# Attention head pipeline: where the split and low parts of the queries and keys of the head two further on stand among the query tiles

## Chip, core and metric

The kernel runs on one core of a Trainium2 chip. The metric is the device time in microseconds of one execution, as a median of several runs. One execution was taken with the hardware profiler; all rows and times of single instructions come from it.

Engines are named as in the profile: PE is TensorE (matrix products), PEld its weight loads, DVE is VectorE, ACT is ScalarE, POOL is GpSimd, SP is SyncE, which issues the transfers.

## Reference

The program is an attention stage, a mixture of experts on its output, and a gated product. Only the first is touched here:

```python
q_bucket = np.sum((np.einsum('bhsd,dk->bhsk', q, proj) > 0) * powers, axis=-1)   # and k_bucket alike
mask = q_bucket[:, :, :, None] == k_bucket[:, :, None, :]
scores = np.where(mask, scale * np.matmul(q, k.transpose(0, 1, 3, 2)), -1000000000.0)
attn = np.exp(scores - np.max(scores, axis=-1, keepdims=True))
attn = attn / (np.sum(attn, axis=-1, keepdims=True) + 1e-09)
return np.matmul(attn, v)
```

There are 2 x 8 heads, sequences of 768, head size 64, float32 throughout. The experts (8, with argmax routing) and the gated product (1536 wide) follow on 1536 tokens.

## The kernel before

**Stages.** The attention stage takes the first third of the span; the experts and the gated product follow. The attention runs over 16 heads (0 to 15) of six query tiles of 128 rows. Its main loop (line 676) makes one pass for each tile, `g = 6 h + t`; "pass t of head h" below is that pass. The loop is a pipeline written out by hand: within pass (h, t)

- TensorE first makes the scores of the *next* tile (`scores`, lines 158 and 159, four products into one PSUM tile `s`), then side work (the products of the previous head's probabilities with V, `av`, line 200, in passes 1, 3 and 5; the hash products of the next head, line 128, in pass 1; the output product of the head before the previous one, line 238, in pass 4), then the transposes of this tile's probabilities in two halves of three (`tp`, line 185). Passes 0 and 2 hold scores and transposes alone.
- VectorE takes the smallest score of the next tile (`mm`, line 164) and makes from it the scale and bias of the exponential (`sb`, line 165, 128x2 values).
- ScalarE makes the exponential `p` of the next tile (line 172), which waits for `sb`. The table `K` says at which of three positions in a pass it is issued: position 0 (ahead of the transposes) in passes 1, 3 and 5, position 2 (behind them) in passes 0, 2 and 4.
- The transposed probabilities are copied out of PSUM to `pt` by ScalarE (line 189) or VectorE (line 191, in passes 1, 2 and 4 for the second half). `tp` has two PSUM buffers, so a half of a tile waits until the same half of the tile before is copied.

Every engine works through its instructions in the order in which the program issues them.

**The split.** Scores are needed to float32 accuracy, and the products run on a format that keeps fewer bits. So queries and keys (`x`, both stacked twice along the partitions) are split into a rounded part and a remainder. For head h + 2, during head h, `split_a(h + 2, i)` (line 100) makes the rounded part on ScalarE, `tq` for queries (i = 0) and `tk` for keys (i = 1), one instruction each (line 103). `split_b(h + 2, i)` (line 107) makes the remainder: for queries VectorE's `bq` (line 115) and a copy on GpSimd (line 116); for keys a subtraction `bk` (line 118) and a copy (line 119), both on GpSimd. The results are first read one head later, by the scores issued in pass 5 of head h + 1.

**Other work around it.** `hash_codes` (line 140) takes the hash products of head h + 1 at position 0 of pass 1: VectorE's `code` (line 142), then four transfers by SP (line 147) that put the codes into rows of `tq` and `tk`. At the end of a head VectorE copies `av` to `o` and forms the reciprocal sums (lines 220 to 225). In pass 4 it scales the output product (`lp`, line 247; `x_all`, line 248), and GpSimd adds `lp` to the router's logits `lg` (line 250; VectorE for the last two heads of a batch). From pass 2 of head 10 on, VectorE also has the router's steps of the first half of the tokens.

**What sets the order.** The entries `sa` and `sb` of `K` list, for queries and keys, the pass and position at which `split_a` and `split_b` are issued; `side` (line 733) looks them up:

```python
K = {..., 'sa': ((2, 2), (4, 1)), 'sb': ((3, 2), (4, 2)), ...}
```

So `tq` is issued at the end of pass 2, `bq` and its copy at the end of pass 3, `tk` in the middle of pass 4 and `bk` with its copy at the end of pass 4.

Of the kernel before, what the change touches and what calls it, by code (L numbers as in the profile page):

```python
# [21 lines left out]
N, DM, E, FF, F2 = 1536, 512, 8, 1024, 1536  # L22
C = 224
GR = ((0, 6), (6, 4), (10, 2))
K = {'se': (2, 0, 2, 0, 2, 0), 'se0': (0, 1, 2, 1, 1, 2), 'ev': (0, 0, 0, 1, 0, 1, 0, 0, 0, 1, 0, 0), 'avl': (), 'oul': 0, 'hml': 0, 'hc': ((0, 0), (0, 2), (1, 1), (2, 1)), 'sa': ((2, 2), (4, 1)), 'sb': ((3, 2), (4, 2)), 'ext': (1, 0, 2, 4, 7, 8), 'hm0': 0, 'hc0': ((1, 0), (1, 2), (3, 0), (4, 1))}
C_ID, C_TRI, C_THR, C_REV, C_TOK, C_IOTA, C_BASE, C_SLOT = 0, 128, 256, 258, 266, 278, 279, 287
CW = C_SLOT + C
FAR = 1024.0
# [4 lines left out]
def attn_moe_kernel(ctx: ExitStack, tc: tile.TileContext, xin, cst, projd, wblk, wmoe, w2in, out):  # L33
# [29 lines left out]
    pos = const.tile([128, 12], F32, name="pos")  # L63
# [24 lines left out]
    NHD = NB * NH  # L88
# [4 lines left out]
    def load(h, first=()):  # L93
        X[h] = xp.tile([128, 2 * S], F32, tag="x", name="x")
        for i in range(2):
            after(nc.sync.dma_start(out=X[h][:, i * S:(i + 1) * S], in_=xin[h, :, i * S:(i + 1) * S]), first)
        V[h] = vp.tile([128, NT, D], F32, tag="v", name="v")
        nc.sync.dma_start(out=V[h], in_=xin[h, :, 2 * S:].rearrange("p (k d) -> p k d", d=D))
# [24 lines left out]
    def hash_mm(h, order=range(4)):  # L123
        p = (ps_m if h or 2 in order else ps_a).tile([128, 512], F32, tag="m" if h or 2 in order else "a", name="m")
        for j in order:
            i = j // 2
            hp_[h, j] = p
            PE.matmul(
                p[32 * j:32 * j + 32, :384], pst[:, 32 * i:32 * i + 32], X[h][:, j * 384:(j + 1) * 384],
                start=True, stop=True, skip_group_check=True,  # L130
            )
# [19 lines left out]
    def scores(g):  # L151
        h, t = divmod(g, NT)
        p = ps_s.tile([128, 2, 512], F32, tag="s", name="s")
        st[g] = p
        qs = slice(t * 128, t * 128 + 128)
        for c in range(2):
            sl = slice(c * 384, c * 384 + 384)
            PE.matmul(p[:, c, :384], T[h, 0][:76, qs], T[h, 1][:76, sl], start=True, stop=False)  # L158
            PE.matmul(p[:, c, :384], B[h, 0][:, qs], B[h, 1][:, sl], start=False, stop=True)  # L159

    def smax(g):
        m = mm[:, g % 4]
        sb = sm.tile([128, 2], F32, tag="sb", name="sb")
        DVE.tensor_reduce(out=m[:, 1:2], in_=st[g][:, :, :384], axis=AX.XY, op=ALU.min)  # L164
        DVE.scalar_tensor_tensor(  # L165
            out=sb, in0=m[:, 1:2].to_broadcast([128, 2]), scalar=BIG / 2, in1=m, op0=ALU.is_le, op1=ALU.mult
        )
        scl[g], nbs[g] = sb[:, 0:1], sb[:, 1:2]
# [9 lines left out]
    def tposes(g, half):  # L178
# [8 lines left out]
        src = ps[:, :384].rearrange("p (a b) -> p a b", a=3)  # L187
        if K["ev"][2 * t + half] == 0:
            ACT.activation(o, src, ACTF.Copy)  # L189
# [5 lines left out]
    def av_step(h, k):  # L195
        if k == 0:
            av[h] = ps_a.tile([128, 512], F32, tag="a", name="av")
        v = V[h][:, k]
        for c in range(2):
            PE.matmul(  # L200
                av[h][c * 64:(c + 1) * 64, :384], v, PT[h][:, k, c * 384:(c + 1) * 384],
                start=(k == 0), stop=(k == NT - 1), skip_group_check=True,
            )
# [261 lines left out]
    def w_load(n, part):  # L465
        if n < 64:
            RAW[n, part] = wraw.tile([128, 512], F32, tag=f"wr{part}", name=f"wr{part}")
            nc.sync.dma_start(out=RAW[n, part], in_=wmoe[n // 8, n % 8, :, part * 512:(part + 1) * 512])
# [126 lines left out]
    with tc.manual_schedule():  # L595
# [49 lines left out]
        def set_up(k):  # L645
            if k == 0:
                split_b(1, 0)
                POOL.tensor_copy(held, pt_[0][:, 0:1])
            elif k == 1:
                split_b(1, 1)  # L650
            elif k == 2:
                POOL.memset(oh, 0.0)
                zero = wraw.tile([128, 512], F32, tag="wr0", name="zero")
                POOL.memset(zero, 0.0)
                zeros.append(zero)
                DVE.tensor_copy(tri, cs[:, C_TRI:C_TRI + 128])
            elif k == 5:
                DVE.tensor_scalar(
                    out=tokc.bitcast(I32)[:, :, 0], in0=cs[:, C_TOK:C_TOK + 12], scalar1=-float(E * C), scalar2=None,
                    op0=ALU.add,  # L660
                )
                DVE.tensor_scalar(
                    out=base2, in0=cs[:, C_BASE:C_BASE + 8], scalar1=1.0 / 128, scalar2=None, op0=ALU.mult
                )
# [6 lines left out]
        extra = {}  # L671
        for at, f in zip(K["ext"], acts):
            extra.setdefault(divmod(at, NT), []).append(f)
        NG = NHD * NT
        qa, qb = (0, 4), (4, 2)
        for g in range(NG):
            h, t = divmod(g, NT)
            if t == 1 and h + 3 < NHD:
                load(h + 3)
            if g + 1 < NG:  # L680
                scores(g + 1)
                smax(g + 1)
            if g < NT:
                set_up(g)
            if 2 * NT <= g < 2 * NT + (E * C + N) // 256:
                for i in (g - 2 * NT,):
                    nc.sync.dma_start(
                        out=xr[i * 256:(i + 1) * 256].rearrange("(p r) d -> p r d", p=128),
                        in_=zeros[0].unsqueeze(1).to_broadcast([128, 2, 512]),
                    )  # L690
            if g == 6 * NT:
                for n in range(4):
                    for part in range(2):
                        w_load(n, part)
            if g == 10 * NT + 1:
                r = router(0)
                todo = [r["s1"], r["s1b"], None, lambda: (r["s2"](), r["s2c"]()), r["s2b"], r["s4"], r["s4b"]]
                for f in r["sc"]:
                    todo += [f, None]
                todo += [r["s4c"], r["s3"], r["s5"]]  # L700
            early, late = [], []
            if h < L:
                if t == (1 if h else 0):
                    early.append(lambda: hash_mm(h + 1))
                if h:
                    for k in AV_AT.get(t, ()):
                        early.append(lambda k=k: av_step(h - 1, k))
                if h > 1 and t == 4:
                    (late if K["oul"] else early).append(lambda: o_out(h - 2))
            elif t < 3:  # L710
                av_step(h - 1, 2 * t)
                av_step(h - 1, 2 * t + 1)
                if t == 0:
                    o_out(h - 2)
                if t == 2:
                    o_evac(h - 1)
            elif t == 3:
                o_out(h - 1)
            else:
                k = 3 * (t - 4)  # L720
                av_group(h, qa, (k, k + 1, k + 2))
                if t == 5:
                    o_evac(h, qa)
            for f in early:
                f()
            if h and h < L and t == 5 and not K["avl"].count(5):
                o_evac(h - 1)
            if g > 10 * NT + 1 and todo:
                f = todo.pop(0)
                if f:  # L730
                    f()

            def side(pos):
                if g + 1 < NG and K["se" if 0 < h < L else "se0"][t] == pos:
                    sexp(g + 1)
                for i in range(2):
                    if h + 2 < NHD and K["sa"][i] == (t, pos):
                        split_a(h + 2, i)
                    if h + 2 < NHD and K["sb"][i] == (t, pos):
                        split_b(h + 2, i)  # L740
                if h < L and (t, pos) == (1, 0):
                    hash_codes(h + 1)

            side(0)
            tposes(g, 0)
            side(1)
            tposes(g, 1)
            for f in late:
                f()
            if h and h < L and t == 5 and K["avl"].count(5):  # L750
                o_evac(h - 1)
            side(2)
            for f in extra.get((h - L + 1, t), ()):
                f()
# [578 lines left out]
```

## Time and profile before

| | |
|---|---|
| median of three runs | 756.61 us (755.6, 756.61, 760.02) |
| the profiled execution | 756.17 us, of which the span of instructions is 754.3 us |
| TensorE busy | 725.7 us, 96% of the span |
| VectorE, ScalarE, GpSimd busy | 528.4, 435.9, 281.1 us |
| TensorE's granted clock | 0.998 of full speed |

The span runs from the first to the last instruction of the program. A busy TensorE is not TensorE at its best, because products overlap and their ends are modelled; how long a pass of the loop takes is read from the starts of its scores (line 158), from one pass to the next. Idle time of the other engines costs nothing by itself. A wait is put down to what came last by the profile.

### The profile page before, as it was taken

The numbers are of one execution on the slowest core, as the hardware profiler recorded it, in microseconds if no ns is written. First come the engines' busy times: TensorE is split into PE (matmuls) and PEld (weight loads), VectorE is DVE, ScalarE is ACT, GpSimd is POOL, SyncE is SP. The second block draws the span as 40 slices with busy tenths as digits, with TensorE's granted clock in tenths as the row PEclk, the third lists the DMA queues.
The fourth block names the chain that finished last, engine by engine and source line by source line (L and its number), as shares of the span: only waits on it lengthen the run. The fifth ranks groups of instructions, "written<-read, shape, count | busy, mean of one in ns | idle before, by whom it ended". The sixth has DMA issues, their size and how long they took to land.

```text
span 754.3 us, 13409 instructions
## 1 busy us (share of the span) xinstructions
PE 725.7 (96%) x4621; PEld 619.7 (82%) x4622; DVE 528.4 (70%) x1033; ACT 435.9 (58%) x945; POOL 281.1 (37%) x319
## 2 busy tenths in 40 slices
PE   8899999999999999999999999999999999999995
PEld 6566666666666689999999999999999998999994
DVE  6777777777877677777778885687767246656641
ACT  5877677776678635666667764444553434344331
POOL 4332223321444256221221104353434476565543
PEclk9999999999999999999999999999999999999999
DMA  6356251112411018778898663646463322212102
GB/s 233 117 200 247 94 189 57 57 57 72 151 36 61 15 70 265 225 223 203 235 353 259 211 197 126 223 155 222 154 222 114 112 100 83 84 44 83 57 1 87
DMA packets 49594, 107.37 MB, mean 142 GB/s; under 512 B 8096, under 2 KB 11504, under 8 KB 47984
## 3 DMA queue, kind: packets, MB, share of 16 engines
q1 hardware_dynamic: 46848, 99.94, 40.8%
q0 software_dynamic: 2304, 6.31, 2.3%
q8 instruction: 38, 0.62, 0.4%
q14 instruction: 36, 0.29, 0.1%
q10 hardware_dynamic: 368, 0.20, 0.1%
HBM read 82.76 MB, written 22.56 MB: 140 GB/s over the span
## 4 chain that ended last, share of the span: by engine, by line
PE 82%; ACT 5%; DVE 5%; issue 3%; DMA 2%; POOL 2%; ACTq 0%; SPq 0%; DVEq 0%; POOLq 0%
PE tp L185 9%; PE av L200 8%; PE y L934 5%; PE acc L1056 4%; PE acc L1055 4%; PE acc L1057 4%; PE s L159 3%; PE s L158 3%; PE h L896 3%; PE h L895 3%; PE h L894 3%; ACT p L172 3%; PE y L935 3%; PE abb L894 2%; PE aba L895 2%
## 5 line engine op out<-in xcount | busy, mean ns | idle before, releaser
L172 ACT ACTIVATE p<-s,sb 128x768 f32<-128x768 f32 x96 | 94.8, 988 | 33.7 <-DVE sb L165 21.1
L164 DVE TENSOR_REDUCE mm<-s 128x1 f32<-128x768 f32 x96 | 91.6, 955 | 27.3 <-PE s L159 25.9
L185 PEld LDWEIGHTS tp<-cs,p 128*128 128x128 f32 x576 | 62.9, 140 | 52.8 <-ACT p L172 24.3
L853 POOL TENSOR_TENSOR pc<-t,pc 128x256 fp32r<-128x256 f32 x86 | 74.7, 892 | 83.3 <-ACT pc L852 83.3
L185 PE MATMUL tp<-cs,p 128*128 128x128 f32 x576 | 83.3, 281 | 16.6 <-ACT pt L189 11.0
L478 DVE TENSOR_TENSOR wl<-wr,wh 128x512 fp32r<-128x512 f32 x125 | 81.3, 689 | 10.0 <-ACT wh L477 5.5
L189 ACT ACTIVATE pt<-tp 128x384 f32<-128x384 f32 x144 | 65.4, 488 | 32.6 <-PE tp L185 32.6
L477 ACT ACTIVATE wh<-wr 128x512 fp32r<-128x512 f32 x128 | 73.8, 624 | 6.8 <-DMA wr<-wmoe 5.9
L934 PE MATMUL y<-hl,wh 128*128 128x448 f32 x224 | 74.9, 378 | 0.2
L158 PE MATMUL s<-tk,tq 76*128 76x384 f32 x192 | 73.1, 381 | 0.3 <-DVE tq L135 0.3
L894 PE MATMUL h<-xh,wh 128*128 128x224 f32 x256 | 71.4, 279 | 0.5 <-ACT wh L477 0.3
L896 PE MATMUL h<-xh,wl 128*128 128x224 f32 x256 | 70.6, 276 | 0.2 <-DVE wl L478 0.2
L895 PE MATMUL h<-xl,wh 128*128 128x224 f32 x256 | 70.2, 274 | 0.3 <-DVE xl L412 0.3
L200 PE MATMUL av<-pt,v 128*64 128x384 f32 x360 | 68.1, 499 | 0.0
L159 PE MATMUL s<-bk,bq 128*128 128x384 f32 x192 | 65.1, 339 | 0.0
L116 POOL CAST bq<-tq 64x768 fp32r<-64x768 f32 x15 | 21.2, 1414 | 112.9 <-ACT tq L103 98.4
L935 PE MATMUL y<-hl,wl 128*128 128x224 f32 x224 | 59.5, 266 | 0.0
L1055 PE MATMUL acc<-h,gh 128*128 128x512 f32 x144 | 56.7, 394 | 0.4 <-ACT gh L1041 0.4
L1056 PE MATMUL acc<-l,gh 128*128 128x512 f32 x144 | 56.8, 394 | 0.0
L1057 PE MATMUL acc<-h,gl 128*128 128x512 f32 x144 | 56.6, 393 | 0.0
L865 POOL TENSOR_TENSOR l<-t,h 128x512 fp32r<-128x512 f32 x24 | 31.0, 1293 | 64.7 <-ACT h L864 64.7
L894 PEld LDWEIGHTS h<-xh,wh 128*128 128x128 f32 x256 | 48.9, 191 | 1.7 <-ACT wh L477 0.5
(225 smaller groups left out, 1868.1 us busy)
## 6 DMA issues: line engine op xcount, KB each, us to landing
wr<-wmoe SPq DMA_DIRECT2D x128, 256.0 KB
r<-w2in SPq DMA_DIRECT2D x12, 1536.0 KB
x<-xin SPq DMA_DIRECT2D x30, 384.0 KB
w<-t SPq DMA_DIRECT2D x36, 256.0 KB
t<-w SPq DMA_DIRECT2D x36, 256.0 KB
xr<-zero SPq DMA_DIRECT2D x13, 512.0 KB
xg<-xr SPq DMA_DIRECT2D x14, 256.0 KB
v<-xin SPq DMA_DIRECT2D x16, 192.0 KB
```

The source lines that it names most:

```text
L158: PE.matmul(p[:, c, :384], T[h, 0][:76, qs], T[h, 1][:76, sl], start=True, stop=False)
L159: PE.matmul(p[:, c, :384], B[h, 0][:, qs], B[h, 1][:, sl], start=False, stop=True)
L164: DVE.tensor_reduce(out=m[:, 1:2], in_=st[g][:, :, :384], axis=AX.XY, op=ALU.min)
L172: ACT.activation(p.rearrange("p (c n) -> p c n", c=2), st.pop(g)[:, :, :384], ACTF.Exp, scale=scl.pop(g), bias=nbs.pop(g), accum_out=sums[ ...
L185: PE.transpose(ps[:, j * 128:(j + 1) * 128], pt_[g][:, k * 128:(k + 1) * 128], ident)
L200: PE.matmul(av[h][c * 64:(c + 1) * 64, :384], v, PT[h][:, k, c * 384:(c + 1) * 384], start=(k == 0), stop=(k == NT - 1), skip_group_check= ...
L894: PE.matmul(ps, wh, xh, start=first, stop=False)
L895: PE.matmul(ps, wh, xl, start=False, stop=False)
L896: PE.matmul(ps, wl, xh, start=False, stop=last)
L934: PE.matmul(p, wh[:, w], hl, start=(f == 0), stop=False, skip_group_check=True)
L1055: PE.matmul(acc[i], h[:, w], wh, start=(f == 0), stop=False)
L1056: PE.matmul(acc[i], h[:, w], wl, start=False, stop=False)
```

## The change

The table `K` gets other entries for the splits, and the old ones stay under new names for head 0:

```diff
-'sa': ((2, 2), (4, 1)), 'sb': ((3, 2), (4, 2)),
+'sa': ((0, 2), (2, 2)), 'sb': ((1, 0), (2, 2)), 'sa0': ((2, 2), (4, 1)), 'sb0': ((3, 2), (4, 2)),
...
-                    if h + 2 < NHD and K["sa"][i] == (t, pos):
+                    if h + 2 < NHD and K["sa" if h else "sa0"][i] == (t, pos):
                         split_a(h + 2, i)
-                    if h + 2 < NHD and K["sb"][i] == (t, pos):
+                    if h + 2 < NHD and K["sb" if h else "sb0"][i] == (t, pos):
                         split_b(h + 2, i)
```

In heads 1 to 13 `tq` is now issued at the end of pass 0, `bq` and its copy at the start of pass 1, `tk`, `bk` and its copy at the end of pass 2. Heads 14 and 15 have no split, and head 0 keeps its places. Instructions and transfers are the same in kind and number. TensorE's order is the same.

VectorE, pass 1 to pass 4 of one of the later heads, before (`mm` and `sb` are those of the next tile, `code` the hash codes, `pt` a transposed half):

```order
L164 TENSOR_REDUCE mm<-s 128x1
L165 SCALAR_TENSOR_TENSOR sb<-mm 128x2
L142 TENSOR_SCALAR code<-m,thr 128x384
L191 COPY pt<-tp 128x3x128
L164 TENSOR_REDUCE mm<-s 128x1
L165 SCALAR_TENSOR_TENSOR sb<-mm 128x2
L191 COPY pt<-tp 128x3x128
L164 TENSOR_REDUCE mm<-s 128x1
L165 SCALAR_TENSOR_TENSOR sb<-mm 128x2
L115 SCALAR_TENSOR_TENSOR bq<-x,tq 64x768
L164 TENSOR_REDUCE mm<-s 128x1
L165 SCALAR_TENSOR_TENSOR sb<-mm 128x2
```

The same stretch of VectorE after the change:

```order
L164 TENSOR_REDUCE mm<-s 128x1
L165 SCALAR_TENSOR_TENSOR sb<-mm 128x2
L115 SCALAR_TENSOR_TENSOR bq<-x,tq 64x768
L142 TENSOR_SCALAR code<-m,thr 128x384
L191 COPY pt<-tp 128x3x128
L164 TENSOR_REDUCE mm<-s 128x1
L165 SCALAR_TENSOR_TENSOR sb<-mm 128x2
L191 COPY pt<-tp 128x3x128
L164 TENSOR_REDUCE mm<-s 128x1
L165 SCALAR_TENSOR_TENSOR sb<-mm 128x2
L164 TENSOR_REDUCE mm<-s 128x1
L165 SCALAR_TENSOR_TENSOR sb<-mm 128x2
```

`bq` has moved from between the `sb` of tiles 4 and 5 to just ahead of `code`.

ScalarE, from the exponentials around the end of pass 2 to those of pass 5, before (`p` is an exponential, `pt` a copy of a transposed half):

```order
L172 ACTIVATE p,sums<-s,sb 128x768
L103 ACTIVATE tq<-x 128x768
L172 ACTIVATE p,sums<-s,sb 128x768
L189 ACTIVATE pt<-tp 128x3x128 x3
L103 ACTIVATE tk<-x 128x768
L172 ACTIVATE p,sums<-s,sb 128x768 x2
L189 ACTIVATE pt<-tp 128x3x128 x4
```

ScalarE from the end of pass 0 to pass 5, after:

```order
L172 ACTIVATE p,sums<-s,sb 128x768
L103 ACTIVATE tq<-x 128x768
L172 ACTIVATE p,sums<-s,sb 128x768
L189 ACTIVATE pt<-tp 128x3x128 x2
L172 ACTIVATE p,sums<-s,sb 128x768
L103 ACTIVATE tk<-x 128x768
L172 ACTIVATE p,sums<-s,sb 128x768
L189 ACTIVATE pt<-tp 128x3x128 x3
L172 ACTIVATE p,sums<-s,sb 128x768 x2
```

`tk` stands where `tq` stood, between the exponentials of tiles 3 and 4, `tq` stands between those of tiles 1 and 2, and the middle of pass 4 holds no split.

On GpSimd the keys' subtraction and copy now come ahead of the addition to the logits instead of behind it.

## Rows read from the trace of the kernel before

**Rows 1.** The page's first line: the span.

```profile
span 754.3 us, 13409 instructions
```

**Rows 2.** TensorE's waits, 30 to 232 us: us in total, times, longest.

```profile
PE tp L185 <- ACT pt L189: 11.0, 14, 1.2
```

**Rows 3.** TensorE in order of time, head 5: start, us, what [idle before].

```profile
93.01 0.42 PE L158 MATMUL s<-tk,tq 76*128 76x384 f32 x1
...
93.80 0.82 PE L185 MATMUL tp<-cs,p 128*128 128x128 f32 x6
94.38 0.42 PE L158 MATMUL s<-tk,tq 76*128 76x384 f32 x1
...
99.51 0.42 PE L158 MATMUL s<-tk,tq 76*128 76x384 f32 x1
...
102.47 0.42 PE L158 MATMUL s<-tk,tq 76*128 76x384 f32 x1
...
104.28 0.93 PE L185 MATMUL tp<-cs,p 128*128 128x128 f32 x6 [0.86 <-ACT pt L189]
104.96 0.42 PE L158 MATMUL s<-tk,tq 76*128 76x384 f32 x1
```

**Rows 4.** ScalarE in order of time, head 5.

```profile
91.60 0.99 ACT L172 ACTIVATE p<-s,sb 128x768 f32<-128x768 f32 x1 [0.59 <-DVE sb L165]
...
96.31 0.83 ACT L103 ACTIVATE tq<-x 128x768 fp32r<-128x768 f32 x1
...
102.76 0.99 ACT L172 ACTIVATE p<-s,sb 128x768 f32<-128x768 f32 x1 [1.10 <-PE tp L185]
```

**Rows 5.** VectorE in order of time, head 5.

```profile
91.56 0.68 DVE L142 TENSOR_SCALAR code<-m,thr 128x384 fp32r<-128x384 f32 x1
93.29 0.56 DVE L191 COPY pt<-tp 128x384 f32<-128x384 f32 x1 [1.05 <-PE tp L185]
...
96.67 0.16 DVE L165 SCALAR_TENSOR_TENSOR sb<-mm 128x2 f32<-128x2 f32 x1
97.17 0.95 DVE L115 SCALAR_TENSOR_TENSOR bq<-x,tq 64x768 fp32r<-64x768 f32 x1 [0.34 <-ACT tq L103]
...
99.31 0.16 DVE L165 SCALAR_TENSOR_TENSOR sb<-mm 128x2 f32<-128x2 f32 x1
99.39 0.26 DVE L247 TENSOR_TENSOR lp<-m,r 128x96 f32<-128x96 f32 x1
...
100.50 0.96 DVE L164 TENSOR_REDUCE mm<-s 128x1 f32<-128x768 f32 x1
101.50 1.15 DVE L165 SCALAR_TENSOR_TENSOR sb<-mm 128x2 f32<-128x2 f32 x1
102.57 0.55 DVE L220 COPY o<-av 128x384 f32<-128x384 f32 x1
```

**Rows 6.** GpSimd in order of time, head 5.

```profile
97.20 1.61 POOL L116 CAST bq<-tq 64x768 fp32r<-64x768 f32 x1 [9.40 <-ACT tq L103]
...
100.82 1.81 POOL L118 TENSOR_TENSOR bk<-x,tk 64x768 fp32r<-64x768 f32 x1 [0.63 <-POOL lg L250]
102.69 0.82 POOL L119 CAST bk<-tk 64x768 fp32r<-64x768 f32 x1
```

**Rows 7.** GpSimd, then VectorE, in order of time, pass 3 of head 2.

```profile
50.15 0.82 POOL L116 CAST bq<-tq 64x768 fp32r<-64x768 f32 x1 [9.40 <-ACT tq L103]
...
50.18 1.60 DVE L115 SCALAR_TENSOR_TENSOR bq<-x,tq 64x768 fp32r<-64x768 f32 x1 [0.41 <-ACT tq L103]
```

**Rows 8.** GpSimd, then VectorE, in order of time, head 10.

```profile
175.96 0.82 POOL L116 CAST bq<-tq 64x768 fp32r<-64x768 f32 x1 [9.38 <-ACT tq L103]
...
176.02 0.77 DVE L165 SCALAR_TENSOR_TENSOR sb<-mm 128x2 f32<-128x2 f32 x1
```

**Rows 9.** SP in order of time, head 5: the transfers of the keys' codes.

```profile
94.08 1.47 SPq L147 DMA_DIRECT2D tk<-code  x2
```

**Rows 10.** The query copies, line 116, 30 to 235 us: ns min/median/max, first and last start.

```profile
L116 POOL CAST bq<-tq x13: 817/1612/1636, 34.8 to 224.1; 64x768 fp32r<-64x768 f32 x13
```

More of the change, by code (lines that the diff above doesn't have):

```diff
@@ L24 @@
 GR = ((0, 6), (6, 4), (10, 2))
-K = {'se': (2, 0, 2, 0, 2, 0), 'se0': (0, 1, 2, 1, 1, 2), 'ev': (0, 0, 0, 1, 0, 1, 0, 0, 0, 1, 0, 0), 'avl': (), 'oul': 0, 'hml': 0, 'hc': ((0, 0), (0, 2), (1, 1), (2, 1)), 'sa': ((2, 2), (4, 1)), 'sb': ((3, 2), (4, 2)), 'ext': (1, 0, 2, 4, 7, 8), 'hm0': 0, 'hc0': ((1, 0), (1, 2), (3, 0), (4, 1))}
+K = {'se': (2, 0, 2, 0, 2, 0), 'se0': (0, 1, 2, 1, 1, 2), 'ev': (0, 0, 0, 1, 0, 1, 0, 0, 0, 1, 0, 0), 'avl': (), 'oul': 0, 'hml': 0, 'hc': ((0, 0), (0, 2), (1, 1), (2, 1)), 'sa': ((0, 2), (2, 2)), 'sb': ((1, 0), (2, 2)), 'sa0': ((2, 2), (4, 1)), 'sb0': ((3, 2), (4, 2)), 'ext': (1, 0, 2, 4, 7, 8), 'hm0': 0, 'hc0': ((1, 0), (1, 2), (3, 0), (4, 1))}
 C_ID, C_TRI, C_THR, C_REV, C_TOK, C_IOTA, C_BASE, C_SLOT = 0, 128, 256, 258, 266, 278, 279, 287
```

## Prediction

> **What bounds the kernel now.** I read the page first, then TensorE's own waits over the attention stage, then one head in order of time, engine by engine. The span is 754.3 us [rows 1]. In the attention stage, from 30 to 232 us, TensorE's waits are nearly all of one kind: transposes that wait for ScalarE's copy of an earlier transpose, 14 times, 11.0 us [rows 2]. The reader should see how regular that is in a head. A pass that holds only scores and transposes takes 1.37 us when nothing waits, from 93.01 to 94.38; the first pass of head 6 holds the same work and takes 2.49, from 102.47 to 104.96, with its transposes held until 104.28 [rows 3]. So a head loses 1.12 us at its first tile.
>
> Follow it back through head 5. ScalarE starts the exponential of tile (6,0) at 102.76 [rows 4], and the transposes follow 1.52 later [rows 3]; in between lie that exponential and the copies queued behind it. Without a stall the transposes would start 0.79 into the pass (93.01 to 93.80), at 103.26 [rows 3], so the exponential would have to start by 101.74. It waits for `sb`, the tiny VectorE operation of line 165, which starts at 101.50 and takes 1.15 instead of the 0.16 of 99.31, until 102.65 [rows 5]. Beside it GpSimd runs the subtraction `bk` from 100.82 for 1.81, to 102.63 [rows 6]: `sb` ends 0.02 later. Two other pairs show who wins. At 50.15 GpSimd's copy starts first, and VectorE's `bq`, started at 50.18, takes 1.60 [rows 7] instead of 0.95; at 97.17 `bq` starts first, and the copy of 97.20 takes 1.61 instead of 0.82 [rows 5 to 7]. The one that starts first holds the other until it ends. The stall is made by where `bk` falls against `sb`, and the change moves `bk`.
>
> **What moves, and its cost.** No operation is added or removed; heads 1 to 13 issue the same splitting steps earlier.
>
> The keys' split. ScalarE's `tk` now stands where `tq` stood, at the end of pass 2, and both are the same operation on 128x768 values, so ScalarE up to the exponential of tile 4 is as it was: `tk` from 96.31 for 0.83, to 97.14 [rows 4]. GpSimd starts 0.06 later, as it does now (97.20): subtraction 97.20 to 99.01, then the copy, 0.06 behind it as at 102.69, from 99.07 to 99.89 [rows 6]. On VectorE `bq` is gone from here, and `sb` of tile 4 is over at 96.83 [rows 5], before the subtraction. But `sb` of tile 5 is ready at 99.31 [rows 5], inside the copy, and a copy holds `sb` too: the one of 176.02 took 0.77 beside a copy that began at 175.96 [rows 8]. So this `sb` ends at 99.91 instead of 99.47. What follows on VectorE, from `lp` at 99.39 to the end of the reduction at 101.46, is a chain with no wait in it [rows 5] and moves by 0.44: reduction from 100.94, `sb` of tile (6,0) from 101.94 at its normal 0.16, to 102.10 instead of 102.65. The gain is **0.55 us** of the 1.12; 0.57 stays. ScalarE is no obstacle: with `tk` gone from pass 4, the exponential of tile 5 waits for its `sb` alone, starts at about 100.0 and is over by 101.1.
>
> The queries' split. `tq` goes behind the exponential of tile 1. ScalarE stands idle for 0.59 before the next exponential, at 91.60 [rows 4]; `tq` takes 0.83; the 0.24 that do not fit are overlapped with its neighbours or put that exponential off by as much, and nothing waits for it yet. On VectorE `bq` comes at about 91.78 for 0.95, and `code`, now 91.56 to 92.24, ends at about 93.3, just when the copy of line 191 can start, 93.29, after 1.05 of idle time [rows 5]. I cost both at nothing, covered by that idle time; it is used up, so with any further delay VectorE passes it on to the next pass. `code` itself now runs beside GpSimd's query copy, which no row shows. Its bounds: nothing, by the copy `o` of 102.57, which also reads PSUM and took 0.55, like line 191's 0.56, beside GpSimd's copy of 102.69 [rows 5, 6]; or held until that copy ends, as `bq` is, 0.65. I take nothing, the nearer row, and keep the rest for the range. Behind `code`, SP's transfers of the codes move by 1.1: their issue ends at 95.55, and the scores that need them start at 99.51 without a wait [rows 3, 9]; 2.9 of 4.0 us stay, and I cost that at nothing. If the landing needed all of it, it would be 1.1 a head.
>
> On `code` the Trainium skill, SBUF — State Buffer, "Who interferes with whom", says that a VectorE instruction with at most one SBUF input, outside its two-port modes, does not contend with GpSimd; by that the cost is nothing, by the upper bound it would be some 0.4 a head. No run here shows it yet.
>
> **The sum.** Heads 1 to 7 and 12: 8 x 0.55 = 4.4. Heads 8 and 9 have the addition to the router's logits on VectorE inside that chain; an operation of the size of `lp` is 0.26 at most and partly overlapped [rows 5], so 0.4 each: 0.8. In head 13 router work stands ahead of `tk`, and what is late there is of another kind; between 0 and 0.55 I take 0.2. Heads 10 and 11 have router work on VectorE in pass 2, which delays `sb` of tile 4: in head 10 it is ready at 176.02, and the subtraction would now begin where the copy began, at 175.96 [rows 8]. Then `sb` waits until 177.8 instead of 176.79, a new stall of 1.0 that eats what the end of the head gives back. I take 0 for both, with -0.5 to +0.7 each. Together 5.4.
>
> Against it stands the race for `bq`. Of 13 query copies the median took 1.61 us and the shortest 0.82, so VectorE is first in most heads [rows 10]; where GpSimd is first, `bq` takes 0.65 longer. That cost nothing before; now `code` and the copy of line 191 follow and end at about 94.5 instead of 93.85, and the last three transposes of the pass that ends at 94.38 need its buffer at about 94.1: 0.4. For one or two heads 0.6. Net 4.8. From the profiled execution, 756.17 (754.3 of span and 1.9 around it), that gives **751.4**. The median of the runs shown, 756.61, is 0.4 above the profiled one.
>
> **The rivals.** *The copy lets `sb` of tile 5 through*, because it starts later or GpSimd yields. Then `sb` of tile (6,0) ends at 101.66 and the stall is gone: ten heads at 1.1, 11.0: 745.2. For it: only one row, 176.02, shows a copy holding an `sb`. Against it: `bq` of 50.18 was held by the same kind of copy. *GpSimd wins the race for `bq` everywhere:* 0.4 in twelve heads, 4.8 of the 5.4: 755.6. For it: the starts are 0.03 apart [rows 5, 6]. Against it: the median of the query copies. *Slower:* the subtraction lands on `sb` of tile 4 in every head, as in head 10. It decides from 0.53 us, the distance from 96.67 to 97.20 [rows 5, 6]. Then that `sb` ends at 99.03, the exponential of tile 4, now started right behind ScalarE's 97.14, starts 2 us later, and the transposes of that tile some 1.8 later; less the 1.1 that the head's end then gives back, 0.7 a head, thirteen heads 9.1: 765.3. Against it: from `sb` of tile 3 on, the work that sets this distance is left alone by the change. *The gain does not reach the end:* heads 10 to 13 eat it, or the stage after the attention starts no earlier: 756.
>
> The race is also where a page bears on the sum. The same section of the Trainium skill's SBUF — State Buffer says that issue order, not the shape of the operation, decides who blocks. The pairs at 50.15 and 97.17 agree: 1.60 and 1.61 us for whichever came second.
>
> **How the numbers follow.** Forecast 0.62 (748.5 to 753.5); copy lets `sb` through 0.08; race lost everywhere 0.15; gain lost later 0.10; slower 0.05. The range leaves out the first rival, the slower one and the edges of the others: 746.5 to 756.0. A measurement of this kernel can tell about 0.5%, 3.8 us, from no change, so faster means below 752.4: nearly all of the forecast (0.53), the full gain (0.08) and a little of the race, 0.64. Slower means above 760: 0.07. The rest, 0.29, is the same.
>
> **What would show it.** Right: `sb` of tile 0 at 0.16 in heads 2 to 10; `sb` of tile 5 at about 0.6, ending 0.02 behind a copy `bk`; the first pass of a head at about 1.9 instead of 2.49, the other passes as long as now; `sb` of tile 4 long in heads 10 and 11 alone. Wrong: `bq` of 1.60 in most heads with a longer pass 2; `code` longer than 0.68; `sb` of tile 4 near 2 us elsewhere; or an attention stage shorter by 5 and a whole that is not.

## Result and the profile after

The changed kernel takes 749.16 us as the median of four runs (747.24, 747.86, 750.46, 750.56), beside 756.87 for the kernel before on the same chip: a ratio of 0.989, with an interval of 0.9849 to 0.9932. The forecast was 751.4 with a range of 746.5 to 756.0. The profiled execution is the one of 750.46 us.

The page's first line, which answers to [rows 1]:

```profile
span 748.6 us, 13396 instructions
```

TensorE's waits over the attention stage, 30 to 228 us (us in total, times, longest), against 11.0 us in [rows 2]:

```profile
PE tp L185 <- ACT pt L189: 3.9, 12, 0.5
```

So 7.1 us of that wait are gone, and what is left comes about once a head as before, but short. Head 5 into head 6 shows why. First TensorE in order of time (start, us, what [idle before]), the pass that took 2.49 in [rows 3]:

```profile
102.09 0.42 PE L158 MATMUL s<-tk,tq 76*128 76x384 f32 x1
...
103.35 0.93 PE L185 MATMUL tp<-cs,p 128*128 128x128 f32 x6 [0.31 <-ACT pt L189]
104.03 0.42 PE L158 MATMUL s<-tk,tq 76*128 76x384 f32 x1
```

The first pass of head 6 lasts from 102.09 to 104.03, 1.94 us, and its transposes wait 0.31 instead of 0.86. Then VectorE, against [rows 5]:

```profile
91.39 0.95 DVE L115 SCALAR_TENSOR_TENSOR bq<-x,tq 64x768 fp32r<-64x768 f32 x1 [0.29 <-ACT tq L103]
92.27 0.66 DVE L142 TENSOR_SCALAR code<-m,thr 128x384 fp32r<-128x384 f32 x1
...
98.93 0.56 DVE L165 SCALAR_TENSOR_TENSOR sb<-mm 128x2 f32<-128x2 f32 x1
...
101.56 0.16 DVE L165 SCALAR_TENSOR_TENSOR sb<-mm 128x2 f32<-128x2 f32 x1
```

And GpSimd, against [rows 6]:

```profile
91.48 1.55 POOL L116 CAST bq<-tq 64x768 fp32r<-64x768 f32 x1 [6.43 <-issue]
96.77 1.82 POOL L118 TENSOR_TENSOR bk<-x,tk 64x768 fp32r<-64x768 f32 x1 [3.74 <-ACT tk L103]
98.65 0.82 POOL L119 CAST bk<-tk 64x768 fp32r<-64x768 f32 x1
```

`sb` of tile (6,0), at 101.56, is back at its 0.16. The subtraction now ends at 98.59, with no `sb` beside it. `sb` of tile 5, which took 0.16 at 99.31 in [rows 5], now takes 0.56: it ends at 99.49, 0.02 behind the keys' copy (98.65 to 99.47). One long hold became one short one.

**Where the time went.** The starts of the scores divide each profiled execution in three: up to the first scores of head 2, from there to those of head 15, and the rest. A head's subtraction meets the `sb` of the next head's first tile, so what the change moves acts on the middle part, head 1's included; only passes 1 to 4 of head 1 lie ahead of it. The ratios are to runs of the kernel before on the chip of each experiment; these have medians of 756.87 (after), 756.21 and 755.53 us.

| kernel | median, us | ratio to before, interval | to head 2 | heads 2 to 14 | rest |
|---|---|---|---|---|---|
| before | 756.87 | | 36.86 | 205.26 | 512.2 |
| after | 749.16 | 0.989 (0.9849 to 0.9932) | 38.41 | 198.08 | 512.1 |
| queries_only | 756.58 | 1.0005 (0.999 to 1.0019) | 40.37 | 204.75 | 511.7 |
| swapped | 745.89 | 0.9859 (0.9843 to 0.9876) | 40.82 | 193.83 | 511.9 |
| copy_late | 748.16 | 0.9886 (0.9857 to 0.9915) | 38.54 | 195.95 | 512.6 |
| copy_twice | 749.16 | 0.9903 (0.9886 to 0.9919) | 37.06 | 198.58 | 511.9 |
| held0 | 748.81 | 0.9902 (0.9867 to 0.9936) | 37.62 | 197.55 | 512.2 |
| swapped_held0 | 743.44 | 0.9825 (0.9798 to 0.9853) | 37.60 | 193.13 | 512.7 |
| keys_next | 745.51 | 0.9857 (0.9825 to 0.9889) | 35.65 | 194.93 | 511.1 |
| sb_one_input | 753.09 | 0.9962 (0.9947 to 0.9977) | 37.89 | 201.41 | 512.2 |
| before_pieces | 747.85 | 0.9893 (0.9874 to 0.9912) | 37.15 | 197.28 | 511.5 |

The middle part lost 7.18 us. The rest is the same within 1.6 us in every kernel: what the attention gains reaches the end. The start does not: from the first scores to those of head 2, heads 0 and 1 took 29.84 us, 2.86 more than before, although head 0 is not changed at all. There a hold of the same kind fell differently in this execution. TensorE, VectorE and GpSimd in order of time, each engine by itself:

```profile
26.31 0.87 PE L185 MATMUL tp<-cs,p 128*128 128x128 f32 x6 [2.24 <-ACT p L172]
...
23.59 1.50 DVE L165 SCALAR_TENSOR_TENSOR sb<-mm 128x2 f32<-128x2 f32 x1
...
23.25 1.82 POOL L118 TENSOR_TENSOR bk<-x,tk 64x768 fp32r<-64x768 f32 x1 [2.60 <-ACT tk L103]
```

Head 0's subtraction starts 0.34 ahead of `sb` of tile (1,0), holds it to 25.09, and TensorE stands for 2.24 us. Behind that its clock is at the lower level for a while. The stretches of the span (us; busy time of PE, PEld, DVE, ACT and POOL; granted clock; share of the DMA engines; GB/s):

```profile
24.00:26.00 2.00, 0.07 (x1) 0.00 (x0) 2.00 (x4) 0.82 (x1) 1.88 (x2) 1.00 0.00 0
26.00:28.00 2.00, 1.69 (x14) 1.30 (x16) 0.26 (x2) 1.36 (x5) 0.00 (x0) 0.90 0.00 0
28.00:30.00 2.00, 2.00 (x11) 0.46 (x12) 1.61 (x3) 2.00 (x4) 0.47 (x1) 0.50 0.00 0
30.00:32.00 2.00, 2.00 (x11) 0.84 (x8) 1.04 (x2) 0.49 (x2) 1.15 (x1) 0.75 0.63 192
```

A granted clock of 0.50 is 1.2 of 2.4 GHz. In the profiled execution of the kernel before, TensorE's longest wait between 20 and 35 us was 0.90 us and the clock stayed at 1.00.

### The profile page after: what moved, and what is told of

Its sections match the earlier page's. It is cut to its first block, busy times and chain, and to the rows that moved or that the text cites. A ratio compares the mean times of both kernels' runs of the same rounds, so it can differ in the third digit from the quotient of the medians.

```text
span 748.6 us, 13396 instructions
## 1 busy us (share of the span) xinstructions
PE 726.0 (97%) x4621; PEld 619.0 (83%) x4622; DVE 521.0 (70%) x1033; ACT 436.1 (58%) x945; POOL 283.3 (38%) x319
## 4 chain that ended last, share of the span: by engine, by line
PE 79%; DVE 9%; ACT 4%; issue 4%; DMA 2%; POOL 1%; SPq 0%; DVEq 0%; ACTq 0%; POOLq 0%
PE tp L185 7%; PE av L200 6%; PE y L934 5%; PE acc L1056 4%; PE acc L1055 4%; PE acc L1057 4%; PE h L896 3%; PE h L895 3%; PE h L894 3%; DVE mm L164 3%; PE s L158 3%; PE s L159 3%; PE y L935 3%; PE abb L894 2%; PE aba L895 2%
## 5 line engine op out<-in xcount | busy, mean ns | idle before, releaser
L907 ACT ACTIVATE hl<-h 128x224 fp32r<-128x224 f32 x64 | 22.8, 357 | 47.8 <-PE h L896 46.9
```

## The experiments

### Which of the two moves brings the gain: queries_only

```diff
-'sa': ((0, 2), (2, 2)), 'sb': ((1, 0), (2, 2)),
+'sa': ((0, 2), (4, 1)), 'sb': ((1, 0), (4, 2)),
```

> Only the queries' split stands at its new place (behind pass 0 and ahead of pass 1); the keys' split is where the kernel before has it, in pass 4. Theory: the stall at the first tile of a head is made by the keys' subtraction beside sb of the next head's tile 0, so it stays: that sb 1.15 us, the first pass of a head 2.49, the total that of the kernel before, 755 to 758 us. Rival, the queries' move itself brings the gain (bq is gone from between the sb of tiles 4 and 5): first pass below 2.1 and 748 to 751 us.

Measured: 756.58 us beside 756.21, the same. `sb` of tile 0 and the subtraction, VectorE and GpSimd of head 5:

```profile
105.54 1.08 DVE L165 SCALAR_TENSOR_TENSOR sb<-mm 128x2 f32<-128x2 f32 x1
...
104.79 1.81 POOL L118 TENSOR_TENSOR bk<-x,tk 64x768 fp32r<-64x768 f32 x1 [0.63 <-POOL lg L250]
```

The hold ends at 106.62, 0.02 behind the subtraction's 106.60, and the first pass of heads 4 to 6 still takes 2.49. So the stall belongs to the keys' place. The queries' move is free in the common head, as costed. Past the start it shows clearly in two heads. Pass 4 of head 10 takes 2.27 instead of 3.03: there the query copy had held `sb` of tile 4 [rows 8], and now it is elsewhere. Pass 2 of head 2 takes 1.85 instead of 1.37: there GpSimd's copy starts ahead of `bq` (48.26 and 48.29), and `bq` takes 1.60.

### Is the hold by the copy worth what it seems: swapped, copy_late, copy_twice

In `swapped` the keys take the early place and the queries the old one; in `copy_late` the keys' copy alone is issued at the end of pass 4; in `copy_twice` it is made twice.

```diff
# swapped
-'sa': ((0, 2), (2, 2)), 'sb': ((1, 0), (2, 2)),
+'sa': ((2, 2), (0, 2)), 'sb': ((3, 2), (1, 0)),
# copy_late
-            copy(b[:64], t[:64])
+            if 1 in part: copy(b[:64], t[:64])
...
+            side(2); 0 < h < NHD - 2 and t == 4 and split_b(h + 2, 1, part=(1,))
# copy_twice
-            copy(b[:64], t[:64])
+            copy(b[:64], t[:64]); h > 2 and copy(b[:64], t[:64])
```

> The two splits change places: the keys' at the end of pass 0 and the start of pass 1, the queries' where the kernel before had them. Theory: on GpSimd the keys' subtraction and copy run from about 91.4 to 94.1 on the clock of the changed kernel's head 5, between the sb of tile 2 (over at 91.10) and that of tile 3 (from 94.62), and hold neither; the query copy runs from 96.8 to 98.4 and is over before sb of tile 5 (98.93). So sb of tile 5 takes 0.16 instead of 0.56, VectorE's chain behind it comes 0.40 earlier, the first pass of a head takes 1.5 instead of 1.94 in some eleven heads, 4.4 us in all: 743 to 746 us. Rival, the copy beside sb of tile 5 costs nothing, and what is left of the stall is of another kind: sb 0.16 and the first pass still 1.94, 747 to 751 us. Second rival, the margin of 0.5 us to sb of tile 3 or tile 5 is not kept in many heads: an sb of 0.5 or more there and 748 us or above.

> The changed kernel with the keys' copy alone put off to the end of pass 4, behind the addition to the logits on GpSimd; the subtraction stays at the end of pass 2. Theory: sb of tile 5 takes 0.16 instead of 0.56 in heads 2 to 7 and 10 to 12, the first pass of a head 1.5 instead of 1.94, while heads 8 and 9, where GpSimd has no addition to wait for, stay as they are: 9 x 0.40 = 3.6 us, 744 to 747 us. Rival, the copy on sb of tile 5 costs nothing: 747 to 751 us with a first pass of 1.94.

> The changed kernel with the keys' copy made twice in a row (the second writes the same values again), in heads 1 to 13. Theory: sb of tile 5 is held by both copies and takes 1.44 instead of 0.56; 0.88 us (0.82 and the 0.06 between two operations) comes back at the first tile of eleven heads, 9.7 us: first pass 2.8, 757 to 760 us, about the kernel before or worse. Rival, the copy holds nothing that matters: 747 to 751 us. Second rival, a tiny sb gets in between the two copies: sb 0.6 and 748 to 751 us.

**swapped** gave 745.89 us. In head 5 GpSimd, VectorE's `sb` of tiles 2, 3 and 5, and TensorE's first pass of head 6 read:

```profile
92.86 1.81 POOL L118 TENSOR_TENSOR bk<-x,tk 64x768 fp32r<-64x768 f32 x1 [6.47 <-ACT tk L103]
94.73 0.82 POOL L119 CAST bk<-tk 64x768 fp32r<-64x768 f32 x1
98.12 1.61 POOL L116 CAST bq<-tq 64x768 fp32r<-64x768 f32 x1 [2.57 <-ACT tq L103]
...
92.24 0.16 DVE L165 SCALAR_TENSOR_TENSOR sb<-mm 128x2 f32<-128x2 f32 x1
...
95.99 0.16 DVE L165 SCALAR_TENSOR_TENSOR sb<-mm 128x2 f32<-128x2 f32 x1
...
100.23 0.16 DVE L165 SCALAR_TENSOR_TENSOR sb<-mm 128x2 f32<-128x2 f32 x1
...
103.39 0.42 PE L158 MATMUL s<-tk,tq 76*128 76x384 f32 x1
...
104.90 0.42 PE L158 MATMUL s<-tk,tq 76*128 76x384 f32 x1
```

All of GpSimd's work on the split stands in gaps between two `sb`, the closest 0.44 us away (95.55 to 95.99). The first pass takes 1.51, and heads 2 to 14 are 4.25 us shorter than after the change, where 4.4 were expected. Not every head gains: in heads 2 and 3 the query copy starts ahead of `bq`, which then takes 1.61 and 1.60 and stands ahead of `sb` of tile 5, and the first passes of heads 3 and 4 stay at 1.90; and in head 10 the query copy is back beside `sb` of tile 4, which takes 0.78. **copy_late** gave 748.16: where the copy was out of the way, `sb` of tile 5 took 0.16 and the first pass 1.58, 0.36 shorter. That happened in seven heads, not the nine expected; with head 14, which became 0.43 longer, heads 2 to 14 are 2.13 shorter. In the heads where the copy was out of the way, both say that the 0.40 of the hold by it is on the path nearly in full (0.44 and 0.36).

**copy_twice** gave 749.16, exactly the time of the changed kernel. My theory (the `sb` waits for both copies, 757 to 760) fell; the second rival is what the trace shows. GpSimd's two copies, then VectorE:

```profile
97.22 0.82 POOL L119 CAST bk<-tk 64x768 fp32r<-64x768 f32 x1
98.10 0.82 POOL L119 CAST bk<-tk 64x768 fp32r<-64x768 f32 x1
...
97.51 0.55 DVE L165 SCALAR_TENSOR_TENSOR sb<-mm 128x2 f32<-128x2 f32 x1
97.98 0.24 DVE L247 TENSOR_TENSOR lp<-m,r 128x96 f32<-128x96 f32 x1
98.15 0.54 DVE L248 TENSOR_TENSOR x_all<-m,r 128x384 f32<-128x384 f32 x1
98.61 0.54 DVE L191 COPY pt<-tp 128x384 f32<-128x384 f32 x1
```

`sb` ends at 98.06, 0.02 behind the first copy, in the 0.06 us before the second one starts. What follows reads PSUM and runs beside the second copy at its usual length. A hold lasts for one GpSimd instruction, not for GpSimd's queue.

### A hold lasts one instruction: before_pieces

If so, the kernel before needs no move: it is enough to cut the subtraction. Here it is the kernel before with `bk` made in four instructions of 192 columns.

```diff
-            (POOL if h else DVE).tensor_tensor(out=b[64:], in0=x[64:], in1=t[64:], op=ALU.subtract)
+            for c in (slice(k, k + n // (4 if h > 2 else 1)) for k in range(0, n, n // (4 if h > 2 else 1))): (POOL if h else DVE).tensor_tensor(out=b[64:, c], in0=x[64:, c], in1=t[64:, c], op=ALU.subtract)
```

> The kernel before, with nothing moved, but the keys' subtraction on GpSimd cut into four instructions of 192 columns each for heads 3 to 15. Doubling the keys' copy showed that a waiting sb gets in when the first of two GpSimd instructions ends. Theory: a hold lasts until the end of the instruction that holds, whatever GpSimd has queued behind it. A piece should take about 0.5 us (1.82 for four), so sb of tile (6,0), which stands 1.15 us behind the start of the last row's hold in the kernel before, is held for at most 0.5 and then goes ahead of the next piece; the first pass of a head takes 1.4 to 1.9 instead of 2.49, and the kernel 744 to 751 us instead of 756, without any move. Rival, GpSimd's next piece, already queued, takes the turn, or the pieces cost much more than a quarter each: sb still 1.0 or longer and 755 us or more.

Measured: 747.85 us beside 756.21, with nothing moved. Two of the four pieces and `sb` of tile (6,0):

```profile
98.95 0.59 POOL L118 TENSOR_TENSOR bk<-x,tk 64x192 fp32r<-64x192 f32 x1 [0.63 <-POOL lg L250]
99.49 0.60 POOL L118 TENSOR_TENSOR bk<-x,tk 64x192 fp32r<-64x192 f32 x1
...
99.63 0.48 DVE L165 SCALAR_TENSOR_TENSOR sb<-mm 128x2 f32<-128x2 f32 x1
```

`sb` goes in at the end of the second piece (100.09; it ends at 100.11) though two more are queued. It takes 0.48 where the whole subtraction held it for 1.15 [rows 5], and the first pass takes 1.82. The four pieces take 2.25 us against 1.81 for one instruction [rows 6]; no `sb` of another tile is held by that. This confirms from the other side that the stall of the kernel before was the length of that one instruction beside that one `sb`.

### What is held: sb_one_input

```diff
-        DVE.scalar_tensor_tensor(
-            out=sb, in0=m[:, 1:2].to_broadcast([128, 2]), scalar=BIG / 2, in1=m, op0=ALU.is_le, op1=ALU.mult
-        )
+        DVE.tensor_scalar(out=sb[:, 0:1], in0=m[:, 1:2], scalar1=BIG / 2, scalar2=-1.0, op0=ALU.is_le, op1=ALU.mult)
+        DVE.tensor_scalar(out=sb[:, 1:2], in0=m[:, 1:2], scalar1=sb[:, 0:1], scalar2=-1.0, op0=ALU.mult, op1=ALU.mult)
```

> The changed kernel with sb made by two VectorE operations of one input tensor each, in place of one with two inputs. Theory: what GpSimd holds is an operation that reads two tensors from SBUF. Then no operation of sb is held anywhere, each takes about 0.16 beside the keys' copy, where the one operation took 0.56; the pair costs some 0.2 us more on tile 5 and on tile 0 in each head, which gives back about what the hold took: first pass 1.8 to 2.0, and 747 to 750 us, with no hold on the sb of tile (1,0) at the start. Rival, any tiny VectorE operation on SBUF is held: the first of the two takes 0.56 beside the copy, first pass 2.2 or more, and 751 to 755 us.

Measured: 753.09 us. The two operations beside the keys' copy, then another one-input operation beside a subtraction:

```profile
98.92 0.82 POOL L119 CAST bk<-tk 64x768 fp32r<-64x768 f32 x1
...
98.95 0.15 DVE L165 TENSOR_SCALAR sb<-mm 128x1 f32<-128x1 f32 x1
99.14 0.21 DVE L166 TENSOR_SCALAR sb<-mm,sb 128x1 f32<-128x1 f32 x1
...
25.34 1.81 POOL L118 TENSOR_TENSOR bk<-x,tk 64x768 fp32r<-64x768 f32 x1 [2.66 <-DVE sb L165]
...
25.49 1.69 DVE L658 TENSOR_SCALAR tokc<-cs 128x12 int32<-128x12 f32 x1
```

The mechanism came out as the theory has it: no operation of `sb` is held anywhere, 0.15 and 0.21 in the middle of the copy. The time did not (747 to 750 expected). The pair makes every tile's scale and bias some 0.2 us later, and that is not free: the first pass takes 2.02 instead of 1.94, and heads 10, 11, 13 and 14 take 0.57, 1.11, 0.30 and 0.62 more than after the change. In head 11, 0.49 of it is pass 2 (1.86), where GpSimd's copy starts ahead of `bq` (184.13 and 184.31); the rest was not followed up. The last two rows forbid the simple reading that one input is enough: `tokc`, one input of 12 values a partition, from SBUF to SBUF, is held to 27.18, 0.03 behind the subtraction; in the kernel before it took 0.17. The Trainium skill, SBUF — State Buffer, "Who interferes with whom", has both: two SBUF inputs contend with a GpSimd instruction that reads SBUF, and an operation like `tensor_scalar` does if it runs in a two-port mode. That `tokc` ran in such a mode, no row here shows.

### The start: held0, swapped_held0, keys_next

In `held0` head 2's subtraction leaves the end of head 0 and waits in head 1 for `sb` of tile (1,1). `swapped_held0` is that with the places of `swapped`. In `keys_next` head h splits the keys of head h + 1 in the early place (`split_a` and `split_b` alike), so head 0 has no keys' split; the loads come one pass later.

```diff
# held0
-                    if h + 2 < NHD and K["sb" if h else "sb0"][i] == (t, pos):
+                    if h + 2 < NHD and K["sb" if h else "sb0"][i] == (t, pos) and (h or not i):
...
-            side(0)
+            side(0); g == NT and (POOL.tensor_copy(held, scl[7]), split_b(2, 1))
# keys_next, K as in swapped
-            if t == 1 and h + 3 < NHD:
+            if t == 2 and h + 3 < NHD:
...
-                    if h + 2 < NHD and K["sb" if h else "sb0"][i] == (t, pos):
-                        split_b(h + 2, i)
+                    if h + 2 - i < NHD and (h or not i) and K["sb" if h else "sb0"][i] == (t, pos):
+                        split_b(h + 2 - i, i)
```

> The changed kernel with one step of the start put off: the keys' subtraction and copy for head 2 leave the end of head 0 and run in head 1, behind a tiny copy on GpSimd that waits for sb of tile (1,1). In the profiled execution of the changed kernel that subtraction held sb of tile (1,0) for 1.50 us, TensorE stood idle for 2.24, and its granted clock then was 0.50 for some 3 us; the two heads took 29.8 us against 27.0 before. Theory: the hold is the cause of both. Then that sb takes 0.16, no idle time of TensorE between 20 and 35 us is over 1.3, no stretch there has a clock below 1, heads 0 and 1 together take 27 to 27.5, and all times lie between 746.5 and 748.5 us. Rival, the clock falls at the start for another reason: a stretch below 1 is seen again, or times at 750 beside times at 747.

> Queries and keys in exchanged places and, in addition, the keys' subtraction and copy for head 2 put off behind sb of tile (1,1). With the places exchanged the median was 745.89 us, and its profiled execution, 748.41, lost 3.9 us in head 1 against the kernel before (18.40 against 14.48). Theory: without the hold at the start 742 to 744 us, and the stage from head 2 to head 15 as long as with the places exchanged alone, 193.8 us. Rival, the subtraction now lands on an sb of head 1: an sb over 1 us between 24 and 32 us and a time of 745 or more.

> Queries and keys in exchanged places, and the keys split one head later: in head h those of head h + 1, in pass 0 and 1 (the loads of x are issued one pass later for it). Head 0 has no keys' split at all. Theory: as with the exchange alone from head 2 on (14.7 us a head), nothing on sb of tile (1,0), no clock below 1: 742 to 744 us. Rival, the codes of the next head, which are now written behind the keys' rounded part, come too late for the scores in pass 5, or the later loads do: a wait of TensorE's weight loads for a transfer in pass 5 or 1, and 745 to 752 us.

**held0** gave 748.81 us (748.09 to 750.51). In its profiled execution `sb` of tile (1,0) takes 0.16, TensorE's longest wait between 20 and 35 us is 0.90, and the clock there is whole. One of the stretches above:

```profile
28.00:30.00 2.00, 2.00 (x16) 0.87 (x17) 1.17 (x2) 2.00 (x5) 1.94 (x2) 1.00 0.00 0
```

Head 1 takes 14.33 us instead of 16.80. Head 0 took 14.73, with a wait of 2.49 ahead of 13.52 for a transfer of constants, and behind that wait the clock fell too: 0.56 and 0.58 in the stretches from 14 to 16 and from 16 to 18 us. So the two heads took 29.06, not 27 to 27.5. And one run of four was still 750.51, so the claim on the times failed. Over all profiled executions: six had the hold at the start (after, queries_only, swapped, copy_late, copy_twice, before_pieces), each with the same 2.24 of idle TensorE, and four of them had the lower clock behind it (not copy_twice and before_pieces); five did not have the hold (before, held0, swapped_held0, keys_next, sb_one_input), and of these held0 alone had the lower clock, behind its other wait. That the hold costs 1.3 us at the start is shown: heads 0 and 1 take 28.23 in copy_twice and 28.30 in before_pieces, which kept the clock, against 26.98 before, and 29.84 after the change, with the lower clock. That the hold is what spreads the times by 3 us is not shown, and a lower clock comes without it. The mean granted clock on record for each run goes with the times: 0.995, 0.995 and 0.994 for the runs of 750.46, 750.56 (after) and 750.51 (held0), 0.996 to 0.998 for the other runs of these two kernels.

**swapped_held0** gave 743.44 us, the fastest here, with heads 2 to 14 in 193.13. An `sb` of head 1 is held for 0.73 at 29.7, short of the 1 us of the rival. **keys_next** gave 745.51, over the 742 to 744 expected: heads 0 and 1 take 27.03, as in the kernel before (26.98), but head 14, which had no keys' split before, takes 16.28 instead of the 15.20 of swapped, with an `sb` of 1.25 us at 225.0 beside its subtraction.

## Why the prediction was right, and where it was not

**The stall and its cause: right.** The hold of `sb` of tile 0 by `bk` was the stall. Moving `bk` alone takes it away (queries_only against after), and so does cutting it (before_pieces).

**The keys' term, 0.55 a head: right in kind and size.** `sb` of tile 5 was to end 0.02 behind the copy at about 0.6, and takes 0.55 to 0.58 in heads 1, 3 to 9, 11 and 12 and 0.47 in head 2. The first pass was to take about 1.9, and takes 1.94. The sum counts a gain to the head whose split moves; it shows in the first pass of the next one. So counted, heads 3, 4, 5, 7 and 12 gained 0.53 to 0.57. The price left over, 0.57 by the prediction, was tested by swapped: 0.44 of it goes with the copy.

**The queries' term, nothing: right.** `code` runs beside the query copy at 0.66 (92.27, with the copy until 93.03), so the lower of its two bounds held. The rule that the prediction cites for it from the Trainium skill (SBUF — State Buffer, "Who interferes with whom") agrees with that row. Passes 1 and 2 are as long as before, save where the race below is lost, and no scores of heads 2 to 15 wait for codes.

**The race for `bq`: right.** GpSimd came first in one head of thirteen, and that head paid 0.48 (pass 2 of 1.85 instead of 1.37), where 0.4 a head, or 0.6 for one or two heads, was taken. GpSimd, then VectorE, head 2:

```profile
45.58 0.83 POOL L116 CAST bq<-tq 64x768 fp32r<-64x768 f32 x1 [6.47 <-ACT tq L103]
...
45.61 1.60 DVE L115 SCALAR_TENSOR_TENSOR bq<-x,tq 64x768 fp32r<-64x768 f32 x1 [0.35 <-ACT tq L103]
```

**Heads 10 and 11 at nothing: wrong.** By the sum's count they gained 0.92 and 0.81. The step that failed is "the subtraction would now begin where the copy began", ahead of `sb` of tile 4. VectorE, then GpSimd, head 10:

```profile
171.85 0.95 DVE L164 TENSOR_REDUCE mm<-s 128x1 f32<-128x768 f32 x1
172.83 0.16 DVE L165 SCALAR_TENSOR_TENSOR sb<-mm 128x2 f32<-128x2 f32 x1
172.91 0.20 DVE L277 TENSOR_REDUCE rt_cm<-rt_cd 128x6 f32<-128x48 f32 x1
173.14 1.62 DVE L278 TENSOR_TENSOR oh<-rt_cd,rt_cm 128x48 bf16<-128x48 f32 x1
...
172.86 1.83 POOL L118 TENSOR_TENSOR bk<-x,tk 64x768 fp32r<-64x768 f32 x1 [3.73 <-DVE mm L164]
```

In the kernel before, VectorE's reduction ahead of the `sb` of [rows 8]:

```profile
174.97 0.95 DVE L164 TENSOR_REDUCE mm<-s 128x1 f32<-128x768 f32 x1
```

`sb` starts 0.03 ahead of the subtraction. In [rows 8] GpSimd was 0.06 ahead. `sb` now follows its reduction by 0.03 (172.80 to 172.83) and not by 0.10 (175.92 to 176.02), and the subtraction starts 0.08 behind ScalarE's `tk` where the copy had started 0.06 behind `tq`. So the order turned on less than 0.1 us, and a forecast from starts 0.06 apart should have held both ends open. The hold then fell on the router's `oh`, 1.62 us, and pass 4 of head 10 takes 2.27, against 2.18 in other heads. Of the 0.92, 0.76 is pass 4 of head 10, and that came with the queries' move alone (queries_only). It was not in the sum at all: the prediction saw the copy hold this `sb` and asked only what would stand there next. In head 11, 0.64 is the keys' term in the first pass of head 12; no `sb` of tile 4 was held there to eat it.

**Other sizes.** Head 6 gained 0.90: `sb` of tile (7,0) had been held for 1.52 in the kernel before, longer than the 1.15 of tile (6,0) which the prediction took for all. Head 1 gained 0.72, and head 13 0.30 against 0.2. Heads 8 and 9 gained 0.32 and 0.35, where 0.4 each was taken for the addition on VectorE. Head 2 gained 0.11, net of the race.

**The start: left out.** Heads 2 to 14 gave 7.18 us where the sum had 4.8: 1.73 of it is heads 10 and 11, taken at nothing, and 0.5 is what heads 1 and 6 gained beyond 0.55 each. Heads 0 and 1 lost 2.86 where the sum had nothing, and the first scores started 1.31 earlier. With 0.07 from the rest that is the 5.7 of the two spans (754.3 and 748.6), near the 4.8 of the forecast because the misses partly cancel; that is luck. The medians differ by 7.7, which is nearer to the middle part alone. The prediction did not ask how the unchanged head 0 varies from one execution to the next.

**The rivals.** That the copy lets `sb` of tile 5 through did not happen: it held in eleven heads. That GpSimd wins the race everywhere did not, nor did the slower case, though in head 10 the two starts were 0.03 us apart. The gain did reach the end.

## What to carry to other kernels

Look for tiny VectorE operations on the critical chain that are far longer than their median, and for the GpSimd instruction that ends 0.02 us before they do: the length of that one instruction, not GpSimd's load, is the price. Put GpSimd's long instructions into the gaps between such operations with some tenths of a us to spare on both sides, or cut them: four pieces gave as much here (747.85) as the move (749.16). Count an order that is settled by less than 0.1 us as open in the sum, and ask of a moved instruction also what it frees where it stood.

## What the runs showed of the hardware

A hold between VectorE and GpSimd lasts for one instruction. A VectorE operation of 0.16 us that waits gets in when the running GpSimd instruction ends, 0.02 us later, also when the next GpSimd instruction is already queued (copy_twice, before_pieces). Not held beside a GpSimd instruction that reads SBUF were: operations on PSUM (`code` 0.66, `x_all` 0.54, `pt` 0.54), a reduction of one SBUF input (`rt_cm` 0.20), and `tensor_scalar` on one value a partition (0.15 and 0.21). Held were operations on two SBUF inputs (`sb`, `bq`, `oh`) and, against the theory of sb_one_input, one `tensor_scalar` with one input of 12 values a partition (`tokc` 1.69).

TensorE's granted clock fell to 0.50, 1.2 of 2.4 GHz, behind an idle time of 2.24 us near the start in four of six profiled executions: in stretches between 26 and 32 us in two (after, copy_late) and between 26 and 34 us in two (queries_only, swapped). In held0 it fell behind an idle time of 2.49 us, between 14 and 18 us. In the other two executions with the same 2.24 us it did not fall; what decides between them stays open.
